# Moving the second half's head sums from TensorE to accumulating DMAs, attention outputs of tiles 8 to 15 behind all MLP products, and eleven LayerNorm tiles on ScalarE

## The chip, the cores and the metric

One core of one Trainium2 chip. The metric is the device time of one execution in microseconds, as the median over several executions. Inputs and outputs lie in HBM; the work between them is done in on-chip memory (SBUF), with PSUM banks for TensorE's results. The engines are TensorE (PE, matmuls), VectorE (DVE, elementwise), ScalarE (ACT, elementwise and tables), GpSimd (POOL; after a few small fills at the start it only issues one queue of DMAs) and SyncE (SP; it issues nearly all loads and stores). Sixteen DMA engines serve all queues of the core.

## The reference

The program mixes two branches by a gate. All sizes are fixed: S = 2048 positions, D = 512 channels, 32 heads of 16, hidden size F = 1792.

```python
def reference(A_x, A_wqkv, A_wo, B_x, B_w1, B_b1, B_w2, B_b2, gate_w):
    x = A_x
    g = sigmoid((x * gate_w).sum(-1, keepdims=True))
    a = A(x, A_wqkv, A_wo)            # attention over 8 keys: positions s, s-2, ... s-14
    b = B(x, B_w1, B_b1, B_w2, B_b2)  # LayerNorm, then an MLP over the positions
    return g * a + (1 - g) * b

# A: q, k, v = x @ wqkv;  logits[w] = sum over 16 channels of q[s] * k[s - 2w];
#    softmax over the 8 values of w;  o = sum over w of attn[w] * v[s - 2w];  o @ wo
# B: h = layernorm(x);  u = gelu(w1^T h + b1)  (2048 -> 1792, over positions);
#    y = w2^T u + b2  (1792 -> 2048)
```

## The kernel before

The kernel is one hand-made program. Each operation is declared with its engine, its estimated duration, what it reads and what it writes. A list scheduler in Python then fixes one static order of operations for each engine, and each engine waits on semaphores where its operands come from another. So an operation that is not ready holds back everything that stands behind it on its engine.

These are the stages that matter here. The order is that of TensorE:

1. Projections q, k, v (products of x^T with wqkv).
2. The MLP's first products (2048 to 1792), called MLP1 below.
3. The MLP's second products (1792 to 2048) in 16 tiles, called MLP2; each tile ends with an output projection `wo` added into the same PSUM bank, which needs the attention result of those positions.

VectorE meanwhile does the attention. The sequence is cut into two halves. For each half it multiplies q with shifted k for four groups of channels and adds them up. What is left is a sum over the four partitions that belong to one head, the *head sum*. In the kernel before, TensorE makes it with 16 small packed matmuls, and ScalarE takes it out of PSUM:

```python
def f_sum(h, b0, with_gate):          # head sums of half h (the first call also makes the gate products)
    def fn(e):
        ...
        for wp in range(4):
            for c in range(4):
                ins = e.matmul(ps[32*c:32*c+32, 4+wp, :], lhsT=RP, rhs=sub(PB[b0], ...),
                               start=True, stop=True, tile_position=(0, 32*c))
        return ins
    return fn

for h in range(2):
    ...                                # q*k products and adds on VectorE, last one is qa..._1
    A("pe",  f_sum(h, b0, h == 0), ..., name="sum%d" % h, prio=-100)
    A("act", act(LOG[h], ps[:, 4:8, :], AF.Copy), ..., name="lev%d" % h)
    # softmax over 8 values: max tree, subtract, exp, sum tree, reciprocal, normalise (nrm)
    A("dve", tt(M4, LOG[h][:, 0:4, :], LOG[h][:, 4:8, :], ALU.max), ..., name="mx4_%d" % h)
    ...
    A("dve", tt(ATT[h], ATT[h], RB, ALU.mult), ..., name="nrm%d" % h)
    for c in range(4):                 # four broadcasts of 512 KB, on GpSimd's queue
        sch.dma("pool", ... e.dma_start(AVW[h] part c, ATT[h] rows repeated 4 times), name="av%d_%d" % (h, c))
```

After the softmax, attention tiles 0 to 7 (256 positions each; 0 to 3 are the first half) follow on VectorE: one multiplication of 4.42 us, then three adds. For the tiles listed in `AVD` the first add is not made by VectorE but by a DMA of 1 MB that adds one piece of SBUF onto another (an *accumulating* DMA, also on GpSimd's queue):

```python
AVD = (3, 4, 5)
def av_mult(u):
    AV(tt(pv, V5 shifted, AVW[h] part c, ALU.mult), 4.4, name="avm%d" % u)
    if u in AVD:
        sch.dma("pool", ... e.dma_start(o_, i_, accum_op=ALU.add, max_dma_last_dim=4096), name="avd%d" % u)
# order: tile by tile; the last adds of a tile in AVD come two tiles later
```

And the order of MLP2: tile i's products, and five tiles later its output projection:

```python
LAG = 5
for i, half in ...:
    PE(f_ph3(i, bank, half), ..., ["w2_%d" % (i // 2)], ...)   # 7 matmuls; needs a piece of w2
    if half == 1 and i >= LAG:
        finish_tile(i - LAG)                                   # wo, eviction, store
```

The weights w1 and w2 come in pieces of about 1 MB on SyncE's queue. They reuse places in SBUF, so a piece is loaded when its place becomes free.

## Time and profile before

The median of the first three executions was 165.28 us (164.96 to 165.71).

| what | value | where to read it |
|---|---|---|
| TensorE busy | 158.6 of 163.0 us (97%) | part 1 of the page |
| VectorE busy | 151.1 us (93%) | part 1 of the page |
| chain of waits | TensorE for 97% of the span | part 4 of the page |
| last q*k add of the second half | ends at 89.78 us | trace, VectorE |
| head sums of that half ready | 94.82 us | trace, ScalarE |
| second softmax ends (`nrm1`) | 112.40 us | trace, VectorE |
| last attention add | 157.41 us | trace, VectorE |

From the page of the kernel before: the span; engine, busy time, its share of the span and instructions; then the busy tenths of TensorE and VectorE and TensorE's granted clock in forty slices; the software queue (GpSimd's) with packets, bytes and share of the DMA engines; and the engines of the chain that ended last.

```profile
span 163.0 us, 1989 instructions
...
PE 158.6 (97%) x793; PEld 77.2 (47%) x808; DVE 151.1 (93%) x126; ACT 70.2 (43%) x100; POOL 12.0 (7%) x36
...
PE   7999999999999999999999999999999999999993
...
DVE  1789999999999999999999999999999999999961
...
PEclk9999999999999999999999999999999999999999
...
q0 software_dynamic: 2512, 9.44, 27.3%
...
PE 97%; ACT 1%; issue 1%
```

TensorE is full from the second slice on, at full clock, and the chain that ended last never leaves it. VectorE is nearly as full, but nothing waits for it. The DMA issues of GpSimd show how the second half's attention is fed. This is its timeline (start, duration, engine, line, operation, count, and in brackets the idle time before and what ended it):

```profile
112.70 2.13 POOL L790 DMA_DIRECT2D arena<-arena  x4 [38.02 <-DVE arena L450]
126.29 1.22 POOL L827 DMA_DIRECT2D arena<-arena  x1 [11.46 <-DVE arena L450]
130.63 1.22 POOL L827 DMA_DIRECT2D arena<-arena  x1 [3.12 <-DVE arena L450]
134.95 1.19 POOL L827 DMA_DIRECT2D arena<-arena  x1 [3.11 <-DVE arena L450]
```

The four broadcasts are issued at 112.70, as soon as the second softmax ends. They landed at 120.52 to 128.20 us. The three accumulating DMAs follow one by one and landed at 134.11, 140.58 and 148.05.

### The profile page before, as it was taken

The page shows a single profiled execution, that of the slowest core. Times are in us where ns is not written, and L with a number is a line of the kernel's source. Part 1 is how long each engine was busy: PE and PEld are TensorE (multiplying, and loading weights), DVE is VectorE, ACT ScalarE, POOL GpSimd, SP SyncE. Part 2 cuts the span into 40 slices and gives each one's busy share as a digit, 9 for nine tenths or more (in the row PEclk, how much of TensorE's full clock was granted, in tenths as well). Part 3 has the DMA queues.
Part 4 walks back from the last instruction along what each step waited for, and adds up shares of the span by engine and source line. Part 5 has one row for each costly group of instructions (what it writes and reads, how often), then busy time and mean ns, then how long its engine had stood idle before and what let it go on. Part 6 is the DMA issues. An engine that isn't in the chain of part 4 may idle for free.

```text
span 163.0 us, 1989 instructions
## 1 busy us (share of the span) xinstructions
PE 158.6 (97%) x793; PEld 77.2 (47%) x808; DVE 151.1 (93%) x126; ACT 70.2 (43%) x100; POOL 12.0 (7%) x36
## 2 busy tenths in 40 slices
PE   7999999999999999999999999999999999999993
PEld 4855555555544344444444344444444444444641
DVE  1789999999999999999999999999999999999961
ACT  3367677666771579662111348011111111111164
POOL 3000030020000000023000000003100222000000
PEclk9999999999999999999999999999999999999999
DMA  5999979729499095999998976981997899991014
GB/s 165 311 268 259 221 183 263 140 38 191 101 277 292 24 242 157 261 290 290 303 245 233 260 188 177 290 209 30 300 243 193 186 207 193 205 216 36 32 59 134
DMA packets 44685, 32.24 MB, mean 198 GB/s; under 512 B 7941, under 2 KB 42245, under 8 KB 44677
## 3 DMA queue, kind: packets, MB, share of 16 engines
q1 hardware_dynamic: 41444, 22.06, 51.6%
q0 software_dynamic: 2512, 9.44, 27.3%
q10 hardware_dynamic: 720, 0.62, 1.2%
q8 instruction: 6, 0.10, 0.2%
q14 instruction: 3, 0.02, 0.0%
HBM read 18.88 MB, written 2.10 MB: 129 GB/s over the span
## 4 chain that ended last, share of the span: by engine, by line
PE 97%; ACT 1%; issue 1%
PE ps L858 30%; PE ps L885 30%; PE ps L649 23%; PE ps L894 8%; PE ps L588 2%; PE ps L551 2%; PE ps L722 1%; ACT arena L453 1%; PE ps L717 1%; PE ps L567 1%; PE ps L604 0%
## 5 line engine op out<-in xcount | busy, mean ns | idle before, releaser
L450 DVE TENSOR_TENSOR arena<-arena 128x4096 bf16<-128x4096 bf16 (+8 forms) x79 | 131.9, 1718 | 1.6 <-ACT arena L453 0.6
L885 PE MATMUL ps<-arena 128*128 128x512 bf16 (+2 forms) x234 | 50.0, 366 | 0.2
L858 PE MATMUL ps<-arena 128*128 128x512 bf16 x218 | 48.5, 379 | 0.3
L453 ACT ACTIVATE arena<-ps,arena 128x512 bf16<-128x512 f32 (+1 forms) x30 | 21.8, 731 | 60.7 <-PE ps L894 37.7
L453 ACT ACTIVATE arena<-ps 128x512 bf16<-128x512 f32 (+3 forms) x53 | 32.9, 629 | 17.4 <-PE ps L649 10.9
L649 PE MATMUL ps<-arena 128*128 128x512 bf16 x173 | 38.0, 379 | 0.2
L885 PEld LDWEIGHTS ps<-arena 128*128 128x128 bf16 x238 | 22.8, 98 | 25.9
L858 PEld LDWEIGHTS ps<-arena 128*128 128x128 bf16 x224 | 21.7, 98 | 26.8 <-issue 0.8
L649 PEld LDWEIGHTS ps<-arena 128*128 128x128 bf16 x176 | 19.9, 113 | 18.0
L894 PE MATMUL ps<-arena 128*128 128x512 bf16 (+2 forms) x67 | 15.6, 366 | 0.1
L453 ACT ACTIVATE arena<-arena 128x16 f32<-128x16 f32 (+5 forms) x10 | 6.7, 678 | 9.7 <-DVE arena L450 9.6
L954 ACT ACT_TABLE_LOAD x7 | 9.0, 1283 | 2.8 <-issue 2.7
L894 PEld LDWEIGHTS ps<-arena 128*128 128x128 bf16 x68 | 6.5, 98 | 7.3
L692 DVE BATCH_NORM_STATS2 arena<-arena 128x6 f32<-128x512 bf16 x16 | 9.9, 679 | 0.1
L790 POOL DMA_DIRECT2D arena<-arena x8 | 4.3, 560 | 75.1 <-DVE arena L450 75.1
L706 DVE TENSOR_SCALAR arena<-arena 128x512 bf16<-128x512 bf16 x16 | 5.3, 404 | 0.0
L827 POOL DMA_DIRECT2D arena<-arena x3 | 3.6, 1209 | 17.7 <-DVE arena L450 17.7
L747 POOL DMA_DIRECT2D arena<-arena x2 | 2.5, 1268 | 30.6 <-DVE arena L692 20.2
L579 DVE CAST arena<-ps 128x256 bf16<-128x256 f32 x4 | 1.6, 422 | 3.2 <-PE ps L567 3.2
L588 PE MATMUL ps<-arena 128*128 128x256 bf16 (+1 forms) x27 | 3.8, 284 | 0.2 <-ACT arena L453 0.2
L551 PE MATMUL ps<-const-bfloat16-1.0 128*128 128x512 bf16 (+1 forms) x9 | 2.7, 483 | 0.8 <-PEq L1004 0.8
L588 PEld LDWEIGHTS ps<-arena 128*128 128x128 bf16 x28 | 2.9, 113 | 0.7 <-DVE arena L579 0.4
(30 smaller groups left out, 14.4 us busy)
## 6 DMA issues: line engine op xcount, KB each, us to landing
arena<-in_B_w_dram SPq DMA_DIRECT2D x7, 1024.0 KB, 6.8
arena<-in_B_w_dram SPq DMA_DIRECT2D x8, 896.0 KB, 9.4
arena<-arena POOLq DMA_DIRECT2D x5, 1024.0 KB, 9.7
arena<-arena POOLq DMA_DIRECT2D x8, 512.0 KB, 11.2
out_dram<-arena SPq DMA_DIRECT2D x15, 128.0 KB, 3.1
arena<-in_A_x_dram SPq DMA_DIRECT2D x3, 512.0 KB, 4.7
arena<-in_A_wqkv_dram SPq DMA_DIRECT2D x2, 256.0 KB, 3.8
arena<-in_A_wqkv_dram SPq DMA_DIRECT2D x1, 512.0 KB, 5.6
```

The lines of the kernel that those rows point to most:

```text
L450: return lambda e: e.tensor_tensor(out=o_, in0=a_, in1=b_, op=op_)
L453: return lambda e: e.activation(out=o_, in_=i_, func=f_, **kw)
L551: ins = e.matmul(ps[:, 7, 0:n_], lhsT=C1, rhs=nc.const_aps.tensor(1.0, (128, n_), BF16), start=True, stop=True)
L588: ins = e.matmul(ps[:, dl, c0:c1], lhsT=sub(WQKV, dt * 3 * D + dl, [(4, 128)]), rhs=XT[:, dt, c0:c1], start=(dt == 0 and hb == 0), stop=(d ...
L649: ins = e.matmul(ps[:, bank, :], lhsT=sub(WQKV, dt * 3 * D + tn * D + dl, [(4, 128)]), rhs=XT[:, dt, sb * 512:(sb + 1) * 512], start=(dt = ...
L692: A("dve", (lambda t_: lambda e: e.bn_stats(out=ST6[:, t_, :], in_=X[:, t_, :]))(t), 0.67, reads=["x%d" % t], writes=["st%d" % t], name="s ...
L706: A("dve", (lambda t_: lambda e: e.tensor_scalar(out=X[:, t_, :], in0=X[:, t_, :], scalar1=col(RSTD, t_), scalar2=col(NMR, t_), op0=ALU.mu ...
L790: prev = sch.dma("pool", (lambda d_, s_: lambda e: e.dma_start(d_, s_))(dst, src), 524288, sch.dsem("av%d_%d" % (h, c)), issue=1.0, reads= ...
L858: ins = e.matmul(ps[:, bank, :], lhsT=W1H[ft // 2][:, st, 128 * (ft % 2):128 * (ft % 2) + 128], rhs=X[:, st, :], start=(st == 0), stop=(st ...
L885: ins = e.matmul(ps[:, bank, 0:c1 - c0], lhsT=W2S[i // 2][:, ft, 128 * (i % 2):128 * (i % 2) + 128], rhs=UT[:, ft, c0:c1], start=(ft == 0) ...
L894: ins = e.matmul(ps[:, bank, 0:c1 - c0], lhsT=OT[:, i // 2, dl, 128 * (i % 2):128 * (i % 2) + 128], rhs=WO[:, dl, c0:c1], start=False, sto ...
L954: e.preload_act_table_set(want)
```

## The change

Intent: TensorE is the bound, so take work from it (the second half's head sums), and take work from VectorE, which is close behind (eleven LayerNorm tiles go to ScalarE). The head sums are made by twelve small DMAs on GpSimd's queue in three rounds, called *folds* here: `fa` (four accumulating, 256 KB) adds partitions 2 and 3 of a head to 0 and 1; `fb` (four plain, 128 KB) moves one of the two into place; `fc` (four accumulating, 128 KB) adds the other. Output projections of tiles 8 to 15 move to the very end of TensorE's work, so that late attention tiles hold back nothing. The weights come in rows of 1 KB instead of 512 B. With this go a new order of attention tiles and new waits (*holds*) before three loads of w2.

```diff
-            for s_ in range(2):
-                qadd(bb[0], bb[2], s_)
-            A("pe", f_sum(h, b0, h == 0), ...)
-            A("act", act(LOG[h], ps[:, 4:8, :], AF.Copy), ..., name="lev%d" % h)
+            def fold(name, o_, i_, acc, nb, reads, writes, after=()):
+                kw = dict(accum_op=ALU.add, max_dma_last_dim=4096) if acc else {}
+                return sch.dma("pool", lambda e: e.dma_start(o_, i_, **kw), ...)
+            if h:
+                for s_ in range(2):
+                    for k_ in range(2):
+                        fas[s_] = fold("fa...", partitions k_ of 4, partitions k_+2 of 4, True, ...)
+                for s_ in range(2):
+                    for k_ in range(2):
+                        for c in (2 * s_, 2 * s_ + 1):
+                            fl = fold(("fb" if k_ == 0 else "fc") + ..., LOG[h] rows, partitions k_ of 4, k_ == 1, ...)
+                folds += [fas[1], fl]
+            else:
+                A("pe", f_sum(b0), ..., name="sum%d" % h)
+                A("act", act(LOG[h], ps[:, 4:8, :], AF.Copy), ..., name="lev%d" % h)
 ... (gate products are now a group of their own, earlier)
         for t in range(NST):
+            if t >= NST - 11:
+                A("act", act(X[:, t, :], X[:, t, :], AF.Identity, scale=col(RSTD, t), bias=col(NMR, t)), ..., name="ln%d" % t)
+                continue
             A("dve", tensor_scalar ..., name="ln%d" % t)
 ...
-            load("w2_%d" % j, W2S[j], w2v[:, :, 256*j:256*j+256], ...)
+            load("w2_%d" % j, W2S[j], w2v[:, 7*(j%2):7*(j%2)+7, 512*(j//2):512*(j//2)+512], ...,
+                 deps={2: folds[0:1], 4: folds[1:2], 6: [avw[1, 1]]}.get(j, []))
 ...
-        AVD = (3, 4, 5)
+        AVD = (2, 4, 5)
+        AVHOLD = {"avm3": msb[1], "ava3": nrm[1]}     # tile 3 behind steps of the second softmax
+        AVORDER = "m0 a0 b0 c0 m1 a1 b1 c1 m2 m3 a3 b3 c3 b2 c2 m4 m5 m6 b4 c4 a6 b6 c6 m7 b5 c5 a7 b7 c7"
 ...
-        LAG = 5
-        (tile by tile, output projection five tiles later)
+        TAILORDER = MLP2 products of tiles 12 to 15, then output projections of tiles 8 to 15
+        (products in groups of four tiles; projections of tiles 0 to 7 follow one group later)
 ... (PSUM banks of MLP1 and MLP2, priorities, the scheduler's own model of DMA time)
```

Besides the folds and the eleven tiles on ScalarE, the change moves operations in the static orders; it adds no other work.

## The prediction

> **What bounds it now.** TensorE. The page gives PE 158.6 us busy of 163.0 (97%), and the chain of waits is PE for 97% of the span. In the timeline a 128x512 matmul starts every 0.216 us from 8.8 to 155 us. VectorE (151.1 us, 93%) is a close second: its last attention add ends at 157.4 us, and the output projection that needs it starts at about 158.6, so it has about 1.2 us to spare. No DMA wait stops PE.
>
> **Removed from PE.** The second half's head-sum group: 16 packed matmuls, 0.98 us in the chain (91.91 to 92.89). The gate products and the first head sum only move. All other PE work is the same in another order. So the floor is 165.3 - 1.0 = 164.3 us.
>
> **Moved off VectorE.** Eleven LayerNorm tiles at 0.32 us each: 3.6 us. ScalarE takes them at about 0.78 us each (what the trace's 128x512 ACTIVATE with two column operands takes; the Trainium skill, "ScalarE: Activation LUTs", section "What ACT_TABLE_LOAD costs", says each pointer operand adds some 93 ns, and the trace agrees: 0.60 without, 0.78 with two). They sit between evacuations: two of 0.60 and one of 0.78, overlapping by 0.09 each, make 1.7 us per 1.73 us of PE. ScalarE just keeps up.
>
> **Added.** Twelve small SBUF-to-SBUF DMAs on the GpSimd queue in three dependent rounds. A 1 MB accumulating DMA took 7.8 to 13.1 us here; the skill's "DMA: Bandwidth & Descriptors" (section on the anatomy of one DMA) gives about 2 us fixed plus size, so I estimate 3 to 5 us for 128 to 256 KB, 10 to 15 for the rounds after VectorE's last query-key add (about 86 us). VectorE has other work (attention tiles 0 to 2) until about 107, so I expect no wait there.
>
> **VectorE's new slack.** Adding trace durations in the new order, the second half's normalisation ends at about 119.4 us (before: 112.4), as the softmax now stands after attention tile 2. The broadcasts (7.8 us to landing before) then land at about 127, while VectorE wants the first at 125.3: a new wait of 1 to 2 us. The accumulating DMA of tile 4 has 8.8 us (7.8 to 10 measured): 0 to 1 us more. VectorE then ends at 155.5 to 158, and PE wants the last tile at about 156.8. The late w2 loads now wait for a broadcast (about 129) and have until 140: enough, narrowly. So most of the 3.6 us saved pays for waits, and PE loses 0 to 1 us of the 1.0 it won.
>
> **Prediction: 164.5 us, 163.8 to 166.0 (8 in 10); faster by over 2%: 0.02, within 2%: 0.94, slower: 0.04.** Two per cent is 3.3 us, three times what leaves PE.
>
> **What would show it.** Right: PE busy down about 1 us; VectorE's LayerNorm group x5; a VectorE wait of 1 to 2 us on a broadcast near 125 us; none on the head-sum DMAs; the last projections without gaps over 1 us. Wrong: VectorE idle at about 107 us for the last fold; PE idle near 140 us (late w2) or before the last projections (late attention).
>
> **What would make it wrong.** GpSimd issues in order: a fold that waits for its partner holds back those behind it, and the folds share the queue with 512 KB broadcasts, which took up to 15.6 us with four in flight. If the three rounds took 25 us, every later step shifts and PE stalls by the excess: 166 to 168 us.

## The result, and the profile after

| | before | after |
|---|---|---|
| median | 165.44 us (164.96 to 165.71, 4 runs) | 177.66 us (177.58 to 178.66, 4 runs) |
| ratio | | 1.0756, 95% interval 1.0709 to 1.0802: slower |
| span of the profiled run | 163.0 us | 175.7 us |
| mean granted TensorE clock | 1.0 | 0.969 |

One run of experiment 10 was slow and is left out of its figures. Ratios are the mean time of one kernel's fast runs over the mean of the other's in the same rounds, so they are not quite the ratio of the medians. Every kernel below gave correct results.

The same lines of the page after the change:

```profile
span 175.7 us, 1985 instructions
...
PE 162.9 (93%) x792; PEld 77.6 (44%) x792; DVE 148.3 (84%) x115; ACT 73.8 (42%) x110; POOL 21.5 (12%) x48
...
PE   7999999999999999999999999999999919619994
...
DVE  1799799999999999999999997497967992699900
...
PEclk9999999999999999999999999999999996966999
...
q0 software_dynamic: 3216, 11.54, 36.1%
...
DMA 41%; DVE 34%; PE 8%; SPq 7%; issue 5%; POOL 2%; ACT 1%; DVEq 0%; POOLq 0%
```

TensorE now has two holes near the end (the 1, and the 6 with the 1 after it, in its row), and its clock falls to 0.6 behind each. VectorE has loose slices from the 25th on (each slice is 4.4 us, so from 105 us). The software queue has 704 packets and 2.1 MB more, all from the folds. The chain has left TensorE: 8% of the span is on it, 41% is on DMAs. This is that chain in order of time (start, duration, what):

```profile
64.58 10.70 DVE arena L452 x7
...
75.58 15.36 DMA arena<-arena
...
92.91 6.14 DMA arena<-arena
...
99.34 7.92 DMA arena<-arena
...
108.45 3.74 DMA arena<-arena
...
123.09 1.24 DVE arena L452
...
125.18 9.47 DMA arena<-arena
...
135.10 22.16 DMA arena<-in_B_w_dram
...
157.31 7.86 PE ps L925 x28
```

It reads as a story. VectorE's adds run to 75.3. The first fold (75.58) takes 15.36 us. A later fold of the first round (issued 92.91) takes 6.14, a second-round fold 7.92, a third-round one 3.74; then come the second softmax, ending at 124.3, one broadcast (9.47), the last piece of w2 (22.16), and only then TensorE. Here is what TensorE was doing at that moment (timeline of TensorE after the change):

```profile
144.69 7.34 PE L925 MATMUL ps<-arena 128*128 128x512 bf16 x28 [3.67 <-DMA arena<-in_B_w_dram]
157.31 7.86 PE L925 MATMUL ps<-arena 128*128 128x512 bf16 x28 [5.28 <-DMA arena<-in_B_w_dram]
```

Both gaps end with the arrival of a piece of w2 (3.67 and 5.28 us). The two groups of 28 matmuls take 7.34 and 7.86 us; in the kernel before, where a matmul starts every 0.216 us and 14 take 3.19 us in this view, 28 would take about 6.2. So TensorE lost 3.67 + 5.28 us in waiting and about 1.1 + 1.7 in slow matmuls, some 11.7 us, most of the 12.7 us between the two spans. (The slow matmuls behind the first gap cost nothing by themselves: the second wait ends when the last piece of w2 lands, at 157.26 us, whatever came before.) The windows of the same trace show why those matmuls are slow (columns: window, its length, busy time and count of PE, PEld, DVE, ACT and POOL, granted clock, DMA share, GB/s):

```profile
98.70:124.00 25.30, 25.30 (x119) 11.47 (x117) 20.50 (x15) 4.87 (x6) 4.11 (x5) 1.00 0.92 216
...
145.60:157.30 11.70, 6.43 (x27) 2.64 (x25) 6.92 (x7) 0.00 (x0) 0.00 (x0) 0.79 0.94 211
157.30:165.20 7.90, 7.89 (x29) 3.32 (x30) 7.87 (x4) 0.00 (x0) 0.00 (x0) 0.74 0.02 5
```

Before the first gap the clock is 1.00, after a gap it is lower. The Trainium skill ("TensorE: Matmul & The Clock Gate", section "Part 1: The HAM clock gate") says that TensorE drops to half clock after an idle window of about 3.4 us and needs about as long in work to come back. The trace agrees: 0.79 and 0.74 are means over windows that mix both states, and in narrower windows of the same trace the clock is 0.50 from 144.4 to 147.7 us, 1.00 from 147.8 to 154.5, 0.50 from 154.7 to 161.4 and 1.00 from 161.5 to 170.

But the weights are only the last link. Had they been on time, the attention would have been late (experiment 8 tests this): VectorE ended its last add at 167.19 us instead of 157.41. The waits of the trace after the change say why (engine, line, what it waited for: total, times, longest):

```profile
DVE arena L452 <- DMA arena<-arena: 10.8, 3, 4.7
PE ps L925 <- DMA arena<-in_B_w_dram: 8.9, 2, 5.3
```

VectorE's three waits on DMAs are 3.56 us for the last fold (the second softmax starts at 112.31 instead of 96.36), 2.53 us for the first broadcast, and 4.68 us for the accumulating add of tile 4. Where the time of the folds went is in GpSimd's timeline (line 786 are the folds, 827 the broadcasts, 866 the adds of attention tiles):

```profile
75.58 0.88 POOL L786 DMA_DIRECT2D arena<-arena  x1 [0.53 <-DVE arena L840]
...
91.23 2.96 POOL L786 DMA_DIRECT2D arena<-arena  x4 [13.30 <-DMA arena<-arena]
96.86 1.73 POOL L786 DMA_DIRECT2D arena<-arena  x2 [2.67 <-DMA arena<-arena]
99.34 1.10 POOL L786 DMA_DIRECT2D arena<-arena  x2 [0.75 <-DMA arena<-arena]
107.80 1.74 POOL L786 DMA_DIRECT2D arena<-arena  x2 [7.36 <-DMA arena<-arena]
...
124.62 2.20 POOL L827 DMA_DIRECT2D arena<-arena  x4 [13.81 <-DVE arena L452]
```

Three things lengthened the rounds, and the last point shows what a fold takes with little else under way:

- The first `fa` (issued 75.58) stood among 512 KB broadcasts of the first half in the same queue, issued at 74.52 and 76.16, and landed at 90.94.
- GpSimd issues in order. Behind it stood the first `fb`, which needs that `fa`. So GpSimd waited 13.30 us, and the `fa` folds of the other part, whose data was ready at 87.12, were issued at 92.31 and 92.91. This order is in part the change's own: its code puts the first `fb` behind the last of the four broadcasts.
- Two second-round folds (99.34 and 99.89) met two loads of w2 released at 97.84 and 98.25 by the hold on the first round. They took 7.9 and 8.3 us. Experiment 2, with more loads of w2 beside them, made the folds slower still.
- The last two third-round folds (107.80 and 108.45), with only the end of a load and the start of an add beside them, took 3.4 and 3.7 us: the size that had been estimated.

From the last add (87.12) to the last sum (112.18) it took 25.1 us. With TensorE it had taken 5.0 us (89.78 to 94.82).

### Why the last piece of w2 took 22 us

It was issued at 135.10, held until a broadcast had landed, and stood in 144 to 153 us beside accumulating adds. The DMA view of the trace (queue, packets, MB, share of the 16 engines; q0 is GpSimd's queue, q1 SyncE's) from 117 to 123 us, where loads of w2 have the engines nearly alone:

```profile
q1 hardware_dynamic: 1772, 1.79, 87.9%
q0 software_dynamic: 33, 0.07, 10.5%
```

And from 145 to 153 us, where the adds of tiles 4 and 5 are under way:

```profile
q0 software_dynamic: 367, 1.44, 89.8%
q1 hardware_dynamic: 368, 0.36, 16.4%
```

Alone, q1 moved 1.79 MB in 6 us, about 300 GB/s. Beside the adds it moved 0.36 MB in 8 us, about 45 GB/s, while q0 kept the engines 90% busy. The packet counts are nearly equal, 367 and 368: one for one. The Trainium skill ("DMA: Bandwidth & Descriptors", section "Queues, rings and completion order") says that each DMA engine goes round the queues that have work, packet by packet. Here a packet of the adds is 4 KB and takes about 0.33 us, and a packet of the loads is 1 KB and takes about 0.05 us, so one for one gives the loads a small share. Experiment 3 below tests this. (The turn is not one for one everywhere; the last section has a stretch where it is not.)

### The profile page after: what moved, and what is told of

Same layout as the page of the kernel before. It is cut to its first block, busy times and chain, and to the rows that moved or that the text cites. A ratio compares the mean times of both kernels' runs of the same rounds, so it can differ in the third digit from the quotient of the medians.

```text
span 175.7 us, 1985 instructions
## 1 busy us (share of the span) xinstructions
PE 162.9 (93%) x792; PEld 77.6 (44%) x792; DVE 148.3 (84%) x115; ACT 73.8 (42%) x110; POOL 21.5 (12%) x48
## 4 chain that ended last, share of the span: by engine, by line
DMA 41%; DVE 34%; PE 8%; SPq 7%; issue 5%; POOL 2%; ACT 1%; DVEq 0%; POOLq 0%
DVE arena L452 31%; DMA arena<-arena 24%; DMA arena<-in_B_w_dram 13%; SPq L495 6%; PE ps L925 5%; DMA arena<-in_A_x_dram 4%; PE ps L934 3%; SPq L496 2%; DVE arena L689 1%; POOL arena L786 1%; ACT arena L455 1%; DVE arena L707 1%; POOL arena L827 0%; DVE arena L680 0%; DVE arena L700 0%
## 5 line engine op out<-in xcount | busy, mean ns | idle before, releaser
L925 PE MATMUL ps<-arena 128*128 128x512 bf16 (+2 forms) x238 | 53.7, 384 | 9.0 <-DMA arena<-in_B_w_dram 8.9
L925 PEld LDWEIGHTS ps<-arena 128*128 128x128 bf16 x238 | 23.4, 101 | 38.4 <-issue 8.8
L455 ACT ACTIVATE arena<-ps 128x512 bf16<-128x512 f32 (+3 forms) x52 | 30.3, 604 | 10.5 <-PE ps L653 4.9
L893 PEld LDWEIGHTS ps<-arena 128*128 128x128 bf16 x224 | 21.8, 98 | 26.6 <-issue 0.4
L653 PEld LDWEIGHTS ps<-arena 128*128 128x128 bf16 x176 | 19.8, 113 | 18.2 <-ACT arena L455 0.4
L455 ACT ACTIVATE arena<-arena 128x512 bf16<-128x512 bf16 (+6 forms) x21 | 15.7, 748 | 25.7 <-DVE arena L452 25.1
L934 PE MATMUL ps<-arena 128*128 128x512 bf16 (+2 forms) x68 | 15.5, 366 | 0.0
L786 POOL DMA_DIRECT2D arena<-arena x12 | 9.6, 877 | 24.6 <-DMA arena<-arena 24.1
L827 POOL DMA_DIRECT2D arena<-arena x8 | 4.7, 606 | 55.2 <-DVE arena L452 55.2
L934 PEld LDWEIGHTS ps<-arena 128*128 128x128 bf16 x68 | 6.5, 98 | 7.2
L866 POOL DMA_DIRECT2D arena<-arena x3 | 4.2, 1399 | 13.9 <-DVE arena L452 13.9
L758 POOL DMA_DIRECT2D arena<-arena x2 | 2.5, 1267 | 27.2 <-DVE arena L689 21.2
## 6 DMA issues: line engine op xcount, KB each, us to landing
arena<-arena POOLq DMA_DIRECT2D x8, 512.0 KB, 11.7
```

What stands on the lines that cost most here:

```text
L455: return lambda e: e.activation(out=o_, in_=i_, func=f_, **kw)
L653: ins = e.matmul(ps[:, bank, :], lhsT=sub(WQKV, dt * 3 * D + tn * D + dl, [(4, 128)]), rhs=XT[:, dt, sb * 512:(sb + 1) * 512], start=(dt = ...
L786: return sch.dma("pool", lambda e: e.dma_start(o_, i_, **kw), nb, sch.dsem(name), issue=1.1, reads=reads, writes=writes, name=name, after= ...
L827: prev = sch.dma("pool", (lambda d_, s_: lambda e: e.dma_start(d_, s_))(dst, src), 524288, sch.dsem("av%d_%d" % (h, c)), issue=1.0, reads= ...
L866: sch.dma("pool", (lambda o_, i_: lambda e: e.dma_start(o_, i_, accum_op=ALU.add, max_dma_last_dim=4096))(pw(0, 4), pw(4, 4)), 1800000, sc ...
L893: ins = e.matmul(ps[:, bank, :], lhsT=w_, rhs=X[:, st, :], start=(st == 0), stop=(st == NST - 1))
```

## The experiments

Ten kernels were run. The texts of expectations use letters for theories: A says that the folded head sums are the cause, by making the second softmax late; C that the three holds on the loads of w2 are; D that the large packets of the accumulating adds starve the loads, and its rival E that the bytes alone decide; a B there stands for the rest of the change (the order of products, weights and attention) costing by itself, whatever the folds do. Two more, L and F, are told where they come up.

### 1. The change with TensorE making the second half's head sums again

```diff
-            if h:                      # folds
+            if h == 2:                 # never
 ...
-            bank = (0, 1, 2, 3, 0, 1, 4, 5, 6, 7, 2, 3, 0, 1)[ft]
+            bank = (0, 1, 2, 3, 0, 1, 2, 3, 0, 1, 2, 3, 0, 1)[ft]   # MLP1 leaves banks 4 to 7 to the sums
```

> The changed kernel with the second half's head sums back on TensorE (16 packed matmuls, 0.98 us), and so no head-sum DMAs and no loads held for them; everything else of the change is kept. Theory A (the three rounds of head-sum DMAs are the root: they push the second softmax 12 us back, and the broadcasts, the late w2 loads and PE follow): softmax of the second half starts near 92 instead of 112.3 us, no PE wait over 1 us near 141 and 152, time 164.8 to 166.5 us. Theory B (the projections of tiles 8 to 15 at the end and the two-ahead attention order are the fault, whoever makes the sums): PE still waits 5 us or more, time above 170 us.

Measured: 171.28 us (170.81 to 172.14), ratio 1.0356 (1.0313 to 1.0399), clock 1.0. About half of the loss went, with every wait for a piece of w2. But it is 5 us over what theory A expected, and in the range of theory B, which blamed the product and attention orders. The two waits that are left, of VectorE and of TensorE:

```profile
DVE arena L452 <- DMA arena<-arena: 8.8, 1, 8.8
...
PE ps L934 <- DVE arena L452: 3.8, 2, 3.2
```

And the issues of GpSimd in the same run, broadcasts (line 827) and the first add (line 866):

```profile
109.67 2.13 POOL L827 DMA_DIRECT2D arena<-arena  x4 [33.45 <-DVE arena L452]
115.88 1.22 POOL L866 DMA_DIRECT2D arena<-arena  x1 [4.08 <-DVE arena L452]
```

VectorE's wait of 8.8 us is one wait, for the accumulating add of tile 2. The change had moved this add from tile 3 to tile 2. With the second softmax early again, the add was issued at 115.88, behind four broadcasts (from 109.67), and landed at 132.97: 17.1 us, where 7.8 were enough in the kernel before. So the changed attention order seems made for a late softmax and does not fit an early one; experiment 5 tests this. Theory A is half shown: the folds are needed for the loss of the weights, but this experiment left something else in.

### 2. The change without the three holds on w2

```diff
-            ..., deps={2: folds[0:1], 4: folds[1:2], 6: [avw[1, 1]]}.get(j, []), after=...)
+            ..., after=...)
```

> The changed kernel without the three holds that keep w2 loads 2, 4 and 6 behind a head-sum DMA or a broadcast. Theory C (the holds are the fault: w2_6 and w2_7 are issued at 134.7 us only because they wait for a broadcast): w2_6 lands before 125, PE's wait of 3.7 us at 141 goes, and the time falls to 167 us or less. Theory A (the head-sum DMAs are the root): w2_6 comes early but VectorE still idles at least 8 us in sum at the last head-sum DMA, the first broadcast and the accumulating DMA, its last add ends at 163 us or later, and the time is 170 to 174 us.

Measured: 178.50 us (177.13 to 179.29), ratio 1.0778 (1.0719 to 1.0837). All pieces of w2 were in time (the last two landed at 124.35 and 135.29), yet nothing was gained: the folds, now among more loads, ended at 118.25 instead of 112.18, VectorE waited 8.63 us for them, and TensorE waited 5.13 us for attention at the end. It also waited 3.36 us (to 129.85) for ScalarE, whose evictions stood behind its steps of the late second softmax in its static order. C falls, and the time is 4.5 us over the range of A too. The holds protect the folds; they shift the loss between weights and attention.

### 3. The change with accumulating adds cut into 1 KB packets

```diff
-    e.dma_start(o_, i_, accum_op=ALU.add, max_dma_last_dim=4096)   # attention adds and folds
+    e.dma_start(o_, i_, accum_op=ALU.add, max_dma_last_dim=1024)
```

> The changed kernel with accumulating DMAs of GpSimd cut into 1 KB packets instead of 4 KB (same bytes). Theory D (the DMA engines take the GpSimd queue's and the other queue's packets in turn, one for one, so a 1 KB weight packet of 46 ns waits for a 4 KB packet of 330 ns and weights crawl at about 45 GB/s): w2_7 takes under 17 us instead of 22.2, landing before 152, and the time falls by 2 to 5 us. Rival E (plain shortage of bandwidth: the bytes decide): w2_7 takes 21 to 24 us as before, time within 1 us of 177.7.

Measured: 179.40 us (178.18 to 180.11), ratio 1.0818 (1.0754 to 1.0882). The DMA view for four microseconds in which adds and the last piece of w2 were both under way:

```profile
q0 software_dynamic: 479, 0.49, 75.6%
q1 hardware_dynamic: 472, 0.45, 41.7%
```

Again one for one, 479 packets against 472, but now of equal size, so the bytes are nearly equal too (0.49 and 0.45 MB). The last piece of w2 took 14.57 us instead of 22.16. The mechanism of D is shown in both directions. The time did not fall, because what the loads won the adds lost: the adds of tiles 4 and 5 took 15.58 and 17.20 us (13.03 and 14.50 in the change), VectorE waited 7.23 us for the first of them, and TensorE waited 5.75 us for attention, besides 3.18 us for the piece of w2 before the last. The expectation for the time was wrong: sharing a full set of DMA engines more evenly is no gain when both users are late.

### 4. The kernel before with eleven LayerNorm tiles on ScalarE, and nothing else

```diff
+            if t >= NST - 11:
+                A("act", act(X[:, t, :], X[:, t, :], AF.Identity, scale=col(RSTD, t), bias=col(NMR, t)), ...)
+                continue
```

> The kernel before with one part of the change alone: eleven LayerNorm tiles on ScalarE. PE is the limit there, so the time stays 165.0 to 165.8 us; VectorE's last attention add ends 3 to 4 us earlier than 157.4. If ScalarE can't keep up beside its evacuations, PE waits in the projections and the time rises by 1 us or more.

Measured: 165.88 us (165.41 to 166.25), ratio 1.0022 (0.9989 to 1.0056): the same. VectorE ended its last attention add at 154.82 instead of 157.41 us, 2.6 us earlier (3 to 4 were expected), and nothing waited for that. This part does what it should and is worth nothing, since TensorE is the bound.

### 5. Experiment 1 with the attention order of the kernel before

```diff
-        AVD = (2, 4, 5)
+        AVD = (3, 4, 5)
-        AVHOLD = {"avm3": msb[1], "ava3": nrm[1]}
+        AVHOLD = {}
-        AVORDER = "m0 a0 b0 c0 m1 a1 b1 c1 m2 m3 a3 b3 c3 b2 c2 m4 ..."
+        AVORDER = "m0 a0 b0 c0 m1 a1 b1 c1 m2 a2 b2 c2 m3 m4 m5 b3 c3 m6 ..."
```

> The run with the second half's head sums on TensorE, now also with the attention order of the kernel before (tiles 3, 4, 5 instead of 2, 4, 5 have an accumulating DMA, and no adds are put off). Left of the change: LayerNorm on ScalarE, the wider weight loads, the products and projections in new order. Theory A (the head-sum DMAs are the root; the 8.8 us that VectorE still waited in the run before are tile 2's accumulating DMA, issued at 115.9 us behind four broadcasts): VectorE has no wait over 2 us after 87 us, its last add ends at 155 to 158 us, time 165.0 to 166.5 us. Rival B (the new product and projection order or the loads' form cost by themselves): 168 us or more.

Measured: 166.20 us (165.98 to 167.54), ratio 1.0059 (1.0014 to 1.0105), clock 1.0, no wait of TensorE over a microsecond. VectorE's only wait for an attention DMA:

```profile
DVE arena L452 <- DMA arena<-arena: 3.2, 1, 3.2
```

The time is inside A's range. Two details are not: the wait is 3.20 us (under 2 expected), and the last add ends at 158.50 us (155 to 158 expected). So everything else that was changed (product order, 1 KB rows, projections at the end, LayerNorm, the one hold that is left) costs together about 0.8 us (by the interval 0.2 to 1.7). Of the 12.2 us, 11.5 come with the folds and with the attention order that was built around them.

### 6. The kernel before with the output projections of tiles 8 to 15 behind all products

```diff
-            if half == 1 and i >= LAG:
+            if half == 1 and LAG <= i < LAG + 8:
                 finish_tile(i - LAG)
 ... (tiles 8 and 9 between the two parts of the last product, 10 to 14 after it)
```

> The kernel before with one part of the change alone: projections of tiles 8 to 15 behind all MLP products. All theories but B: PE stays the limit, 165.0 to 166.0 us. B: 168 us or more.

Measured: 165.66 us (165.50 to 165.70), ratio 1.0008 (0.9986 to 1.0031): the same, as expected.

### 7. The change, repaired: folds first, w2 early, attention order of before

GpSimd's queue gets a fixed order in which the folds stand before the last two broadcasts of the first half, in the order in which their data is expected. The last two pieces of w2 go to places in SBUF that are free early. The second softmax stands behind attention tile 1 instead of behind the multiplication of tile 2.

```diff
+        "pool": "... av0_0 fa1_00 fa1_01 av0_1 fb1_0 fb1_1 fa1_10 fa1_11 fc1_0 fc1_1 fb1_2 fb1_3 av0_2 fc1_2 fc1_3 av0_3 ..."
+        "dve":  "... qa1_10_1 avm0 ava0 avb0 avc0 avm1 ava1 avb1 avc1 mx4_1 mx2_1 mx1_1 msub1 avm2 ... nrm1 ..."
-        W2S = [..., w2view("X", NFT * 256), w2view("S4")]
+        W2S = [..., w2view("W1", 2 * W1N), w2view("XT")]      # places of pieces 0 and 1
-        deps={2: folds[0:1], 4: folds[1:2], 6: [avw[1, 1]]}
+        deps={2: [last fb]}
-        AVD = (2, 4, 5)
+        AVD = (3, 4, 5)
```

> The changed kernel with its head-sum DMAs kept but freed of what delayed them: on GpSimd's queue they stand before the third and fourth broadcast of the first half, loads w2_2 and on wait for the second round of the last sums, w2_6 and w2_7 go to the places of w2_0 and w2_1 (free at 104 and 110 us) instead of waiting for the second softmax, and the attention order is that of the kernel before, with the softmax after tile 1. Theory A with D (sums are late because they queue behind 512 KB broadcasts and behind each other, weights because they alternate with 4 KB packets): last sum lands at 100 to 104 us instead of 112.2, VectorE waits under 2 us there, w2_7 lands before 130, no PE wait over 1 us, time 164.2 to 166 us. If three rounds of DMA inherently take 25 us: last sum at 110 or later, time above 168.

Measured: 177.55 us (177.04 to 178.41), ratio 1.0746 (1.0700 to 1.0792): as slow as the change. The repair did what it was built for. The first fold took 5.97 us instead of 15.36. The last sum landed at 106.13 (112.18 in the change; 100 to 104 expected), still 19.0 us after the last q*k add, VectorE waited 1.81 us for it, and no piece of w2 was waited for. The loss came back elsewhere, as the waits of VectorE and TensorE show:

```profile
DVE arena L461 <- DMA arena<-arena: 13.2, 3, 8.8
...
PE ps L945 <- DVE arena L461: 9.4, 1, 9.4
```

The longest of VectorE's waits is 8.8 us for the add of tile 3, issued at 125.69 behind the four broadcasts of 120.75 and landed at 145.47, 19.8 us later. TensorE stood still for 9.4 us until tile 3's attention was there. So not only the folds' own duration matters. The second softmax still ended at 120.45.

### 8. The change with the last two pieces of w2 in early places, and nothing else

```diff
-        W2S = [..., w2view("X", NFT * 256), w2view("S4")]
+        W2S = [..., w2view("W1", 2 * W1N), w2view("XT")]
-        deps={2: folds[0:1], 4: folds[1:2], 6: [avw[1, 1]]}
+        deps={2: folds[0:1], 4: folds[1:2]}
```

The orders on TensorE, VectorE, ScalarE and GpSimd are the same as in the change, operation by operation.

> The changed kernel with w2_6 and w2_7 loaded into the places of w2_0 and w2_1, free of the broadcast and of the second softmax; all else, the orders on all engines too, as in the change. It takes PE's wait for weights away and leaves VectorE's lateness. If the weights alone are the loss (12 us: waits 9.0, cold clock 3.1): 165 to 167 us. If VectorE is nearly as late (last add at 167.2 us with the weights late): PE's waits at 141 and 152 go, it waits for attention near its end instead, and the time is 171 to 175 us.

Measured: 172.14 us (171.36 to 173.72), ratio 1.0414 (1.0350 to 1.0477), as expected. The two pieces landed at 127.92 and 132.23. TensorE's only long wait is now for attention (timeline of TensorE):

```profile
160.81 7.22 PE L934 MATMUL ps<-arena 128*128 128x512 bf16 x28 [5.60 <-DVE arena L452]
```

The window behind that wait, with the columns of the windows above:

```profile
160.80:164.00 3.20, 3.19 (x8) 1.20 (x9) 3.17 (x2) 0.78 (x1) 0.00 (x0) 0.50 0.00 0
```

So taking the late weights away wins 5.5 us of the 12.2 (177.66 less 172.14). The other 6.7 go with the wait of 5.60 us for attention and the slow matmuls behind it. After this wait of 5.60 us the clock is exactly 0.50, which is the half clock that the skill's page names.

### 9. The repaired kernel with TensorE's head sums: is it lateness or the folds' traffic?

Experiment 7 left two theories. L: the second softmax ends too late, and what must follow it takes its time whatever came before. F: the folds' transfers take the DMA engines from others, or their waits stop someone. This kernel has no folds, but VectorE's order of experiment 7 word for word, so its second softmax is late on purpose. (Its expectation calls experiment 7 "the eighth run".) TensorE's and ScalarE's orders, which experiment 7 had fixed too, were left to the scheduler here.

```diff
-            if h:
+            if h == 2:                 # never: head sums by TensorE, as in experiment 1
-        "pool": "... av0_0 fa1_00 fa1_01 av0_1 ... av0_3 av1_0 ..."
+        "pool": "... av0_0 av0_1 av0_2 av0_3 av1_0 ..."
         "dve": (unchanged)
```

> The eighth run (folds first, last two MLP2 loads in freed places, second softmax behind attention tile 1) with ONE thing changed: the second half's head sums are made by TensorE again, so there are no fold transfers at all; VectorE's order is word for word that of the eighth run, so the second softmax still comes behind tile 1. Theory L (it is the lateness of the second softmax that costs, because GpSimd's queue needs about 30 us after it): the first softmax operation starts near 104.5 us instead of 106.26, its last one ends near 118.5, the accumulating add of tile 3 still lands some 27 us later (143 to 145), VectorE waits 6 to 9 us for it, and the time is 174 to 177 us. Theory F (the folds' own traffic or waits cost the time): 165 to 168.5 us, with no wait of VectorE over 4 us.

Measured: 174.66 us (173.87 to 175.07), ratio 1.0566 (1.0545 to 1.0587): inside L's range and far from F's. (The add of tile 3 landed at 142.50 us, a little before the 143 to 145 of L.) The waits of VectorE and TensorE:

```profile
DVE arena L461 <- DMA arena<-arena: 10.1, 2, 7.5
...
PE ps L945 <- DVE arena L461: 5.4, 1, 5.4
```

And GpSimd's issues, broadcasts (line 838) and the first add (line 877):

```profile
118.98 2.14 POOL L838 DMA_DIRECT2D arena<-arena  x4 [43.23 <-DVE arena L461]
123.92 1.22 POOL L877 DMA_DIRECT2D arena<-arena  x1 [2.81 <-DVE arena L461]
```

The sums were ready long before they were used, the softmax started at 104.49 and ended at 118.68, and the same train of waits followed: the add of tile 3, issued at 123.92, landed at 142.50 (18.6 us), VectorE waited 7.5 us and TensorE 5.4. Against experiment 5 (166.20 us), which has the same sums, the same order of attention tiles and the softmax 9.7 us earlier, the lateness costs 8.5 us in this attention order, which is that of the kernel before. (The places of the last two pieces of w2 differ too, but neither kernel waits for them.) Experiment 7, with the folds, takes 2.9 us more than experiment 9; its softmax also ends 1.8 us later, so this is not the folds' traffic alone.

### 10. Experiment 5 with the start of the k projections of before

```diff
+        kb0 = [bank_() for dl in range(2)]      # two k projections by halves of the contraction
+        for k_ in range(2):
+            for dl in range(2):
+                PE(f_proj(1, dl, 0, kb0[dl], 2 * k_, 2 * k_ + 2), ..., XT0 + ["wk%d" % k_], ...)
```

> The run with TensorE sums and the attention order of before (166.2 us, 0.6% over before) plus before's start of the k projections (two tiles by halves, so that the first does not wait for the second half of the k weights). If what is left of the slowdown lies in that wait at the start: 165.2 to 165.8 us. If it lies elsewhere (the order of the products, the extra wait of tile 3): 166.0 to 166.6.

Measured: 166.15 us (165.78 to 166.59, the five fast runs of six; the sixth, 168.46, was slow), ratio 1.0045 (1.0027 to 1.0063). The projections start at 8.95 us instead of 9.57, and the time is no different. The last 0.7 us over the kernel before does not lie in this wait; where it lies stays open.

## Why the prediction was wrong, and where it was right

The runs put side by side. Times are in us from the start of the profiled span; the last column is the median.

| kernel | head sums | second softmax ends | last attention add ends | time |
|---|---|---|---|---|
| before | TensorE | 112.40 | 157.41 | 165.44 |
| 4: LayerNorm tiles only | TensorE | 108.55 | 154.82 | 165.88 |
| 6: late projections only | TensorE | 113.21 | 158.22 | 165.66 |
| 5: sums on TensorE, order of before | TensorE | 108.95 | 158.50 | 166.20 |
| 10: the same, k projections of before | TensorE | 108.69 | 158.30 | 166.15 |
| 1: sums on TensorE, order of the change | TensorE | 109.38 | 164.52 | 171.28 |
| 9: late on purpose | TensorE | 118.68 | 165.37 | 174.66 |
| 7: repaired folds | folds | 120.45 | 168.34 | 177.55 |
| 8: early places for w2 | folds | 124.59 | 164.94 | 172.14 |
| after | folds | 124.31 | 167.19 | 177.66 |
| 3: small packets | folds | 126.05 | 171.21 | 179.40 |
| 2: no holds | folds | 130.38 | 170.54 | 178.50 |

From the end of the second softmax to the last attention add it takes 40 to 55 us. In the kernel before it takes 45.0 us, and all of this is VectorE's own work, without a wait for a DMA. That work covers the train of transfers that hangs on the softmax: four broadcasts (15 to 19 us from the first issue to the last landing), then two or three adds of 1 MB in the same queue, each 7.8 us at best. Where more attention work stands before the softmax, less is left behind it: about 36 us in the change and in experiments 7, 8 and 9 (the time less the waits). The train does not get shorter with it, so VectorE waits on the train: 7.2 us in the change, 11.3, 4.7 and 10.1 us in experiments 7, 8 and 9.

With TensorE wanting the last tile at about 157 us, the second softmax has to end by about 113 to 117 (an estimate, from 157 less 40 to 44). The kernel before ends it at 112.40. The kernels with folds end it between 120 and 130. But its end does not set the time alone. Experiment 1 ends it early and loses by the order of its adds. Experiment 8 ends it 5.9 us later than experiment 9, and its last add comes 0.4 us earlier: in its attention order, that of the change, two adds follow the broadcasts, and in that of experiment 9 three. So the 8.5 us of experiment 9 are not a measure for the change itself; what lateness alone costs in the change's own order was not measured.

Point by point:

- **"TensorE bounds it", "the floor is 164.3": right as far as it goes.** Experiments 4 and 6 move nothing, as TensorE is the bound. The gain of 0.98 us can't be seen: it is lost in 12 us of waits and slow matmuls.
- **"ScalarE just keeps up": right.** A LayerNorm tile took 0.81 us there (0.78 predicted), VectorE's LayerNorm group fell to x5, and experiment 4 shows that it costs nothing.
- **"10 to 15 [us] for the rounds after VectorE's last query-key add": the term that was mis-sized.** It was 25.1 us. The size of a single fold was right when it had the engines nearly to itself (3.4 to 3.7 us). What was missing was everything around it: 15.4 us for the first one among broadcasts, 5 us from the time the data was ready to the issue behind a fold that was not, and 8 us instead of 3.5 beside loads of w2. The last paragraph of the prediction names just this case, including the 25 us; it gave it too little weight.
- **"VectorE has other work (attention tiles 0 to 2) until about 107, so I expect no wait there": this is the step in the reasoning that failed.** The wait itself was small (3.56 us). But the work that covered the folds was the work that in the kernel before covered the broadcasts and the first add. It can cover only one of the two. Experiment 9 shows, without any fold and in the attention order of before, a price of 8.5 us for doing that work before the softmax instead of after it. The prediction did see the normalisation at 119.4 and the broadcast wait of 1 to 2 us (2.53 measured, to 132.89), but went on as if the queue were free after it. In its own sum, VectorE waits 0 us for the folds, 1 to 2 for the broadcast and 0 to 1 for the add, and ends at 155.5 to 158. The trace has 3.56, 2.53 and 4.68 us, a softmax that ends at 124.31 instead of 119.4, and the last add at 167.19.
- **"The accumulating DMA of tile 4 has 8.8 us (7.8 to 10 measured): 0 to 1 us more": too small.** It took 13.03 us, with a wait of 4.68. The 7.8 to 10 were two of the three adds in the kernel before; the third had taken 13.09 there already.
- **"The late w2 loads ... have until 140: enough, narrowly": wrong.** They were issued at 134.67 and 135.10, not 129, and took 9.9 and 22.2 us, so they landed at 144.56 and 157.26. The last alternated packet for packet with 4 KB packets of the adds. Experiment 8 puts 5.5 us on the two together.
- **"PE stalls by the excess: 166 to 168 us", said for the case of 25 us: too small by 10 us.** The delay reached TensorE by two paths, the attention and the weights that were tied to a broadcast, and the slow matmuls behind the last gap cost about 1.7 us more, which the prediction did not count at all.

What stays open: the 0.7 us that experiments 5 and 10 keep over the kernel before; and whether some third order, with folds, could end the second softmax by 115 us. The best that was tried had its sums at 106 us. No kernel tried here beats the one before, and with TensorE busy for 97% of the span, this change could win at most about the 0.98 us that it takes from it (an estimate, as in the prediction).

## What to carry to other kernels

Before moving a small step from a full engine to DMAs, look at what starts when that step ends: if a long train of transfers hangs on it, the step's latency can count almost in full (8.5 us for a softmax 9.7 us later in experiment 9), even where the engine that waits seems to have other work, because that work was already the cover of the train. Work backwards from the end ("the last tile is due at 157, what hangs on the softmax takes at least 40, so it must end by 117") before adding up what is saved. And size a DMA by what its queue and the DMA engines carry at that moment: in-order issue, neighbours with larger packets and a hold tied to the same train each multiplied a correct estimate of the single transfer.

## What the Trainium skill lacked or had wrong

- "DMA: Bandwidth & Descriptors", section "Anatomy of one DMA — SWDGE (gpsimd) path": its fit of about 2.0 us plus bytes at 436 GB/s gives, as an estimate, 2.3 us for 128 KB and 4.4 us for 1 MB. Accumulating DMAs from SBUF to SBUF took 3.4 to 3.7 us for 128 KB and 7.8 us at best for 1 MB. The page has no figure for accumulating ones. In the stretch 145 to 153 us they were 90% busy at about 180 GB/s.
- The same page, section "Queues, rings and completion order": it states the alternation by packet, which the runs confirm (367 to 368, 479 to 472), but not what follows for unequal packets: a load in 1 KB packets fell from about 300 to about 45 GB/s beside adds in 4 KB packets. The turn is not always one for one: in the kernel before, from 114 to 120 us, broadcasts had 214 packets and a load in 512 B packets 1552.
- The same page, section "Rules for kernel authors": "Issue the DMA early, do compute, wait on its semaphore late" lacks the warning that the compute can be cover for only one train of DMAs (8.5 us in experiment 9).
- "TensorE: Matmul & The Clock Gate", section "Part 1: The HAM clock gate": nothing was found wrong (clock 0.50 after a gap of 5.60 us). A gap of 3.19 us left the clock at 1.00 in experiment 1, and one of 3.18 us was followed by a mean of 0.74 in experiment 3; this fits the free-running window that the page describes, so a gap near 3.4 us can go either way.
